# Two edits at the passage from the mixing stage to the experts: where the low parts of x are computed, and which PSUM banks the first projections use

## The chip, the cores and the metric

The kernel runs on one core of a Trainium2 chip. The metric is device microseconds of one execution, lower is better. Five engines work side by side and are kept in step by semaphores: TensorE (PE in the profile; its weight loads are PEld), VectorE (DVE), ScalarE (ACT), GpSimd (POOL) and SyncE (SP), which issues the loads from and stores to memory.

## The reference, cut to what matters

Three stages follow each other on a tensor of 4 batches, 576 tokens and 512 channels. First, sparse attention over 8 heads (half of them local, half strided) gives x. Second, a mixing stage: rotation angles `theta = x @ w_theta`, products of x with their cosine and sine, mixing over tokens, a channel product with a ReLU. Third, four attention experts with a gate:

```
logits = x @ w_gate                      # two of the four experts are kept
for e in range(4):
    q, k, v = x @ wq[e], x @ wk[e], x @ wv[e]
    a  = softmax(causal(q @ k.T / 8))    # 576 x 576 per batch
    ye = a @ v @ wo[e]
    out += gate[e] * ye
```

## The kernel before, in words

x is held transposed, as `X[b]`: 4 chunks (c = 0 to 3) of 128 channels by 576 tokens, for each of the batches b = 0 to 3. Nearly every product is made of three matmuls: each fp32 factor is split into a high part rounded to the matmul's format and a low part, the rest (`mm3`, lines 263 to 266: high by high, high by low, low by high).

`split_act` (L252) splits one chunk of 128 by 576. The high part is a copy: on ScalarE (L256) once all four batches have been split for the mixing stage, on VectorE before that. The low part is a subtraction (L260), and line 259 chooses its engine. `xsplit` is a dictionary that holds one entry for each batch already split. It is empty at the first split, and holds 4 entries when the splits for the experts are made; for those, VectorE takes chunks 0 and 2 and GpSimd takes chunks 1 and 3. Four splits are made for the experts: batch 0 at line 443, inside the last part of the mixing stage; batches 1, 2 and 3 in `project_v` (L465), that is, inside the experts' work for the batch ahead.

The mixing stage ends with `channels(3)` (L361), whose tiles `g` are evicted by VectorE at L371. Then the PSUM pool of that stage is closed and the pool `ps2` (L450) opens, with 8 banks in four tags: `acc` with 2 (projections, output products), `s` with 3 (scores), `t` with 2 (transposes of the weights p), `o` with 1 (attention output).

Line 707 runs nine units of work before the first attention: five of `project_v(0)` (a unit is 12 matmuls for 128 tokens and 260 columns: V of four experts and the gate's logits) and four of `project_qk(0, 0)` (12 matmuls each, 288 tokens of q or of k for two experts). A unit takes one PSUM bank of tag `acc`, which is free again when it has been evicted. For V that is a copy on ScalarE (L494), a subtraction on VectorE (L495) and a copy of the logits on VectorE (L496) into the tile `lg`, which GpSimd has cleared (L469); the fifth unit is copied out whole first (L490), because it serves two batches. For q it is, for each of two halves, a scaled copy on ScalarE (L546) and a subtraction on VectorE (L547); for k, a copy on ScalarE (L550), a subtraction on VectorE (L551) and a copy on GpSimd (L552). GpSimd's queue holds six clearings of the `klow` tiles (L460) ahead of the first clearing of `lg`.

In the experts' stage, `attention` takes one expert of one batch through five tiles of tokens: scores `s` (L596 to L599), row maxima (L601), exponentials (L612), scaling (L619, GpSimd or VectorE), transposes into `tp` (L622), the split of the transposed weights (L630, L631), and the products with V (L574, L578). Between them, lists named `fill` place units of the projections for the batch to come and of the output of the batch behind, each behind the scores of its tile. The order of every engine's instructions is fixed when the program is built, by a planner that simulates the engines; an engine works through its own list strictly in order.

Of the kernel before, what the change touches and what calls it, by code (L numbers as in the profile page):

```python
# [12 lines left out]
F32 = mybir.dt.float32  # L13
# [10 lines left out]
B, S, DM, HD, NE = 4, 576, 512, 64, 4  # L24
# [23 lines left out]
def fused_kernel(ctx: ExitStack, tc: tile.TileContext, ql, kl, vl, qs, ks, vs, wth, wtk, wch, wqk, wvg, wo, out):  # L48
    nc = tc.nc

    def f(ap):
        return ap.bitcast(F32)
# [32 lines left out]
    for rw in (LQ, RQ):  # L85
        t = wb.tile([128, 2, rw], BF16, name=f"twice{rw}")
# [165 lines left out]
    def split_act(x, name):  # L252
        hi = act.tile([128, S], F32R, tag="ahi", name=f"{name}_hi")
        lo = act.tile([128, S], F32R, tag="alo", name=f"{name}_lo")
        if len(xsplit) == B:
            nc.scalar.copy(hi, x)  # L256
        else:
            nc.vector.tensor_copy(hi, x)  # L258
        eng = nc.vector if not xsplit or len(xsplit) == B and name.endswith(("0", "2")) else nc.gpsimd
        halved[name] = eng.tensor_tensor(lo, x, f(hi), op=ALU.subtract).ins  # L260
        return hi, lo

    def mm3(ps, ahi, alo, bhi, blo, first, last):
        nc.tensor.matmul(ps, ahi, bhi, start=first, stop=False)  # L264
        nc.tensor.matmul(ps, ahi, blo, start=False, stop=False)  # L265
        return nc.tensor.matmul(ps, alo, bhi, start=False, stop=last)  # L266

    def split_x(b):
        return [split_act(X[b][:, c, :], f"x{len(xsplit)}_{b}_{c}") for c in range(4)]

    sins, turns = {}, {}
    xsplit, trig, z = {}, {}, {}
# [177 lines left out]
    ps2 = ctx.enter_context(tc.tile_pool(name="ps2", bufs=2, space=PSUM))  # L450


    xproj, vs, qks, moved = {}, {}, {}, []
    identr, mask_cr = (cw.tile([128, 128], F32R, name=name) for name in ("identr", "mask_cr"))
    nc.vector.tensor_copy(identr, ident)
    nc.vector.tensor_copy(mask_cr, mask_c)
# [7 lines left out]
    def project_v(b):  # L464
        xproj[b] = xsplit[0] if b == 0 else split_x(b)  # L465

        vc = cp.tile([128, NT, NE, 2, HD], F32R, tag="vc", name=f"vc_{b}")
        lg = cp.tile([128, NT, 4], F32, tag="lg", name=f"lg_{b}")
        nc.gpsimd.memset(lg, 0.0)  # L469

        nc.gpsimd.memset(f(vc[64:128, NT - 1]), 0.0)
        vs[b] = vc, cp.tile([128, NT, 4], F32, tag="gt", name=f"gt_{b}")
        if b % 2 == 0:

            xe_hi, xe_lo = (cp.tile([128, S], F32R, tag=tag, name=f"xe{tag}_{b}")[:, :512].rearrange(
                "p (c w) -> p c w", c=4) for tag in ("ohi", "olo"))
            for i in range(2):
                x, sl = X[b + i][:, :, 512:S], slice(64 * i, 64 * i + 64)
                nc.scalar.copy(xe_hi[:, :, sl], x)
                nc.vector.tensor_tensor(xe_lo[:, :, sl], x, f(xe_hi[:, :, sl]), op=ALU.subtract)  # L480

        def unit(t):
            w, t0 = TW[t], 128 * t
            if t < 4 or b % 2 == 0:
                pv = ps2.tile([128, 512], F32, tag="acc", name=f"pv_{b}_{t}")
                for c in range(4):
                    xhi, xlo = (v[:, t0:t0 + 128] for v in xproj[b][c]) if t < 4 else (xe_hi[:, c, :], xe_lo[:, c, :])
                    mm3(pv[:, :260], xhi, xlo, wvg_hi[:, c, :], wvg_lo[:, c, :], c == 0, c == 3)
                if t == 4:
                    nc.scalar.copy(v_end, pv[64:128, :260])  # L490
            else:
                pv = v_end
            v = pv[:w, :256].rearrange("p (e d) -> p e d", e=NE)
            nc.scalar.copy(vc[:w, t, :, 0, :], v)  # L494
            nc.vector.tensor_tensor(vc[:w, t, :, 1, :], v, f(vc[:w, t, :, 0, :]), op=ALU.subtract)  # L495
            nc.vector.tensor_copy(lg[:w, t, :], pv[:w, 256:260])  # L496
            if t == NT - 1:
                gates(b, lg)

        return unit  # L500

    def gates(b, lg):
        gt = vs[b][1]

        cnt = cp.tile([128, NT, 4], F32, tag="cnt", name=f"cnt_{b}")
        cmp = cp.tile([128, NT, 4], F32, tag="cmp", name=f"cmp_{b}")
        nc.gpsimd.memset(cnt, 0.0)
        for j in range(4):
            for e0, e1, op in ((0, j, ALU.is_gt), (j + 1, 4, ALU.is_ge)):
                if e0 < e1:  # L510
                    nc.vector.tensor_tensor(cmp[:, :, e0:e1], lg[:, :, j:j + 1].to_broadcast([128, NT, e1 - e0]),
                                            lg[:, :, e0:e1], op=op)
                    nc.vector.tensor_tensor(cnt[:, :, e0:e1], cnt[:, :, e0:e1], cmp[:, :, e0:e1], op=ALU.add)
        mx = cp.tile([128, NT, 2], F32, tag="mx", name=f"mx_{b}")
        nc.vector.tensor_reduce(mx[:, :, 0], lg, axis=AX.X, op=ALU.max)
        nc.vector.tensor_tensor(lg, lg, mx[:, :, 0:1].to_broadcast([128, NT, 4]), op=ALU.subtract)
        nc.scalar.activation(gt, lg, AF.Exp)
        nc.vector.tensor_scalar(cnt, cnt, 1.5, None, op0=ALU.is_lt)
        nc.vector.tensor_tensor(gt, gt, cnt, op=ALU.mult)
        nc.vector.tensor_reduce(mx[:, :, 1], gt, axis=AX.X, op=ALU.add)  # L520
        nc.vector.tensor_scalar_add(mx[:, :, 1], mx[:, :, 1], 1e-9)
        nc.vector.reciprocal(mx[:, :, 1], mx[:, :, 1])
        nc.vector.tensor_tensor(gt, gt, mx[:, :, 1:2].to_broadcast([128, NT, 4]), op=ALU.mult)
# [3 lines left out]
    def project_qk(b, m):  # L527
        q = [cp.tile([128, S], F32R, tag="q", bufs=6, name=f"q_{b}_{m}_{i}") for i in range(2)]
        k = [cp.tile([128, S], F32R, tag="k", bufs=5, name=f"k_{b}_{m}_{i}") for i in range(2)]
        kl = klow[(2 * b + m) % 3]  # L530
        for i in range(2):
            qks[b, 2 * m + i] = (q[i], k[i], kl[i])

        def unit(part, n):
            ms = slice(256 * m + 128 * part, 256 * m + 128 * part + 128)
            sc = 1.0 / math.sqrt(HD) if part == 0 else 1.0
            sl = slice(HALF * n, HALF * (n + 1))
            pq = ps2.tile([128, 512], F32, tag="acc", name=f"pq_{b}_{m}_{part}_{n}")
            for c in range(4):
                mm3(pq[:, :HALF], wqk_hi[:, c, ms], wqk_lo[:, c, ms], xproj[b][c][0][:, sl], xproj[b][c][1][:, sl],  # L540
                    c == 0, c == 3)
            for i in range(2):
                own, other = slice(64 * i, 64 * i + 64), slice(64 - 64 * i, 128 - 64 * i)
                ps = pq[own, :HALF]
                if part == 0:
                    nc.scalar.activation(q[i][own, sl], ps, AF.Copy, scale=sc)  # L546
                    nc.vector.scalar_tensor_tensor(q[i][other, sl], ps, sc, f(q[i][own, sl]), op0=ALU.mult,  # L547
                                                   op1=ALU.subtract)
                else:
                    moved.append(nc.scalar.copy(k[i][own, sl], ps).ins)  # L550
                    nc.vector.tensor_tensor(kl[i][own, sl], ps, f(k[i][own, sl]), op=ALU.subtract)  # L551
                    nc.gpsimd.tensor_scalar(k[i][other, sl], f(k[i][own, sl]), 1.0, 1.0, op0=ALU.mult, op1=ALU.mult)  # L552

        return unit
# [235 lines left out]
```

## Time and profile before

| quantity | value |
|---|---|
| runs | 560.03, 561.43, 562.27 us, median 561.43 |
| profiled execution | 563.35 us, span 561.5 us, mean granted clock 0.979 |
| busy PE, PEld | 532.7 us (95%), 509.5 us (91%) |
| busy DVE, ACT, POOL | 398.9 us (71%), 316.3 us (56%), 199.2 us (35%) |
| passage and experts' stage | about 344.5 us to the end |

The span runs from the first to the last instruction. A busy PE in this table says that matmuls were in flight, not that they ran at full rate: where the granted clock is 0.5 the same matmul takes about twice as long. The mixing stage fills TensorE almost without gaps; the gaps lie in the first 80 us, in the passage and in the experts' stage.

### The profile page before, as it was taken

Reading aid. Unit: us, or ns where it says so; the run is one execution under the profiler, and the core shown is the slowest. Engines: PE = TensorE matmul, PEld = TensorE weight load, DVE = VectorE, ACT = ScalarE, POOL = GpSimd, SP = SyncE. Lnnn points to the kernel's source line nnn. Section 1 sums busy time; section 2 is a strip of 40 time slices with the busy share of each in tenths; the row PEclk is TensorE's granted clock in tenths of the full one; section 3 lists DMA queues with packets and bytes.
Section 4 is the critical chain, followed back from the end, with each engine's and each line's share of the span. In section 5 each row is a group of like instructions: output and inputs, shape, how many; then the busy total and the mean of one; then the engine's idle time right before and its main releaser. Section 6 shows DMA issues by size and latency. Waiting matters only on the chain.

```text
span 561.5 us, 12501 instructions
## 1 busy us (share of the span) xinstructions
PE 532.7 (95%) x4536; PEld 509.5 (91%) x4536; DVE 398.9 (71%) x1210; ACT 316.3 (56%) x904; POOL 199.2 (35%) x285
## 2 busy tenths in 40 slices
PE   6878889999999999999999999989999999999988
PEld 5768889998999999999999998879989999999977
DVE  4858998585856476865456543797988898888972
ACT  4957975436362154352245421585688667767872
POOL 3330013230634112561006443264455444625451
PEclk9959999999999999999999999998999999999998
DMA  9938153360202131000100011000001001100112
GB/s 292 331 99 312 43 169 125 116 232 20 87 17 72 33 123 39 24 24 5 53 0 1 12 48 39 1 1 2 1 10 57 22 2 44 43 2 11 40 37 85
DMA packets 20389, 37.53 MB, mean 67 GB/s; under 512 B 2904, under 2 KB 12296, under 8 KB 20328
## 3 DMA queue, kind: packets, MB, share of 16 engines
q1 hardware_dynamic: 20328, 36.73, 20.1%
q8 instruction: 36, 0.59, 0.4%
q14 instruction: 25, 0.20, 0.1%
HBM read 32.01 MB, written 4.72 MB: 65 GB/s over the span
## 4 chain that ended last, share of the span: by engine, by line
PE 68%; DVE 15%; ACT 6%; POOL 2%; issue 2%; DMA 2%; DVEq 0%; POOLq 0%; ACTq 0%
PE y L264 6%; PE y L266 6%; PE y L265 6%; PE av L242 4%; PE s L189 3%; PE th L264 3%; PE th L266 3%; PE g L264 3%; PE tp L622 3%; PE g L266 3%; PE g L265 3%; PE th L265 3%; PE tp L219 2%; DVE nm L601 2%; PE o L578 2%
## 5 line engine op out<-in xcount | busy, mean ns | idle before, releaser
L264 PE MATMUL y<-wtk_hi,zhi 128*128 128x288 f32 x288 | 85.8, 299 | 1.3 <-DVE X L349 0.8
L265 PE MATMUL y<-wtk_lo,zhi 128*128 128x288 f32 x288 | 85.7, 298 | 0.0
L266 PE MATMUL y<-wtk_hi,zlo 128*128 128x288 f32 x288 | 85.5, 298 | 0.0
L216 POOL TENSOR_TENSOR p<-p,sm 128x288 f32<-128x288 f32 (+2 forms) x48 | 33.3, 700 | 144.2 <-DVE sm L215 57.8
L619 POOL TENSOR_SCALAR p<-p,sm,gt 128x256 f32<-128x256 f32 (+1 forms) x64 | 45.2, 709 | 53.7 <-DVE sm L617 35.2
L612 ACT ACTIVATE p<-s,nm 128x128 f32<-128x128 f32 (+2 forms) x96 | 49.5, 518 | 14.4 <-DVE nm L601 7.9
L264 PEld LDWEIGHTS y<-wtk_hi,zhi 128*128 128x128 f32 x288 | 54.0, 188 | 2.1 <-DVE X L349 1.3
L334 POOL TENSOR_TENSOR zlo<-cs,zhi 128x512 fp32r<-128x512 f32 (+1 forms) x30 | 35.8, 1205 | 54.0 <-DVE zhi L330 43.3
L265 PEld LDWEIGHTS y<-wtk_lo,zhi 128*128 128x128 f32 x288 | 54.1, 188 | 0.1
L266 PEld LDWEIGHTS y<-wtk_hi,zlo 128*128 128x128 f32 x288 | 54.0, 188 | 0.2
L264 PE MATMUL th<-wth_hi,x_hi 128*128 128x256 f32 (+1 forms) x160 | 47.5, 298 | 2.7 <-DVE cs L288 2.2
L601 DVE TENSOR_REDUCE nm<-s 128x1 f32<-128x128 f32 (+2 forms) x96 | 44.3, 469 | 5.4 <-PE s L599 4.4
L265 PE MATMUL th<-wth_lo,x_hi 128*128 128x256 f32 (+1 forms) x160 | 45.7, 287 | 0.0
L266 PE MATMUL th<-wth_hi,x_lo 128*128 128x256 f32 (+1 forms) x160 | 45.3, 288 | 0.1
L223 ACT COPY pt<-tp 96x384 f32<-96x384 f32 (+2 forms) x44 | 20.9, 477 | 41.9 <-PE tp L219 41.5
L189 PE MATMUL s<-k,q 128*108 128x54 f32 (+2 forms) x320 | 43.1, 277 | 1.4 <-DMA k<-in_kl 1.4
L189 PEld LDWEIGHTS s<-k,q 128*108 128x108 f32 (+1 forms) x320 | 40.9, 198 | 3.4 <-issue 3.2
L260 POOL TENSOR_TENSOR x_lo<-X,x_hi 128x576 fp32r<-128x576 f32 x20 | 29.6, 1484 | 33.1 <-DVE x_hi L258 26.4
L264 PE MATMUL pq<-x_hi,wqk_hi 128*128 128x288 f32 x128 | 39.8, 311 | 1.0 <-DVE q L547 0.7
L264 PE MATMUL g<-u_hi,wch_hi 128*128 128x288 f32 x128 | 38.7, 303 | 1.4 <-DVE X L371 1.4
L631 DVE TENSOR_TENSOR ptlo<-tp,pthi 128x128 fp32r<-128x128 f32 (+4 forms) x80 | 37.7, 479 | 1.1 <-ACT pthi L630 0.6
L265 PE MATMUL pq<-x_lo,wqk_hi 128*128 128x288 f32 x128 | 37.9, 296 | 0.0
(172 smaller groups left out, 1704.8 us busy)
## 6 DMA issues: line engine op xcount, KB each, us to landing
X<-in_wtk SPq DMA_DIRECT2D x18, 287.8 KB
q<-in_qs SPq DMA_DIRECT2D x8, 594.0 KB
q<-in_ql SPq DMA_DIRECT2D x8, 576.0 KB
v<-in_vl SPq DMA_DIRECT2D x24, 144.0 KB
out_t<-X SPq DMA_DIRECT2D x20, 128.0 KB
k<-in_kl SPq DMA_DIRECT2D x8, 304.0 KB
k<-in_ks SPq DMA_DIRECT2D x8, 288.0 KB
X<-in_wth SPq DMA_DIRECT2D x8, 255.8 KB
```

What stands on the lines that cost most here:

```text
L189: nc.tensor.matmul(s[:rm, i * kw:i * kw + w], qt[:, j0 + i, :], kt[:, k0:k0 + w], start=False, stop=i == n - 1)
L216: nc.gpsimd.tensor_tensor(tiles(p), tiles(p), each(sm), op=ALU.mult)
L242: nc.tensor.matmul(av[64 * h:64 * h + 64, c0:c0 + wi], vg[:w, i, h, :], pt[:w, i, h, :wi], start=True, stop=True)
L260: halved[name] = eng.tensor_tensor(lo, x, f(hi), op=ALU.subtract).ins
L264: nc.tensor.matmul(ps, ahi, bhi, start=first, stop=False)
L265: nc.tensor.matmul(ps, ahi, blo, start=False, stop=False)
L266: return nc.tensor.matmul(ps, alo, bhi, start=False, stop=last)
L334: halved[b, h] = eng.tensor_tensor(lo, zf, f(hi), op=ALU.subtract).ins
L601: nc.vector.tensor_reduce(nm[:w, t + ci:t + ci + 1], s[:w, :c1 - c0], axis=AX.X, op=ALU.max, negate=True)
L612: nc.scalar.activation(p[:w, c0:c1], scs[ci][:w, :c1 - c0], AF.Exp, bias=nm[:w, t:t + 1], scale=1.0, accum_out=acc)
L619: eng.tensor_scalar(p[:w, :kn], p[:w, :kn], sm[:w, t:t + 1], gt[:w, t, e:e + 1], op0=ALU.mult, op1=ALU.mult)
L631: nc.vector.tensor_tensor(dst(ptlo), src, f(dst(pthi)), op=ALU.subtract)
```

## The change

Two edits. The low parts of all splits for the experts go to VectorE, chunks 1 and 3 as well, in all four batches. And the projections take their PSUM tile from a function `place`, which hands out the tags `t, t, s, s, s, acc, acc` to the first seven units, in the order in which units are written, and `acc` to all later ones. Nothing else differs in the source; the planner orders the new program anew.

```diff
@@ split_act
-        eng = nc.vector if not xsplit or len(xsplit) == B and name.endswith(("0", "2")) else nc.gpsimd
+        eng = nc.vector if len(xsplit) in (0, B) else nc.gpsimd
@@ before project_v
+    free = ["t", "t", "s", "s", "s", "acc", "acc"]
+
+    def place(name):
+        tag = free.pop(0) if free else "acc"
+        return ps2.tile([128, 512], F32, tag=tag, bufs=3 if tag == "s" else 2, name=name)
+
@@ project_v, unit
-                pv = ps2.tile([128, 512], F32, tag="acc", name=f"pv_{b}_{t}")
+                pv = place(f"pv_{b}_{t}")
@@ project_qk, unit
-            pq = ps2.tile([128, 512], F32, tag="acc", name=f"pq_{b}_{m}_{part}_{n}")
+            pq = place(f"pq_{b}_{m}_{part}_{n}")
```

## Rows read from the trace of the kernel before

**Rows 1.** What TensorE waited for from 344 us on: total, times, longest, in us.
```profile
PE pv L266 <- DVE x_lo L260: 2.1, 2, 1.2
PE pq L264 <- DVE q L547: 0.7, 1, 0.7
```
**Rows 2.** Timeline of TensorE in the passage: start, duration, in brackets idle time before.
```profile
345.11 0.39 PE L264 MATMUL pv<-wvg_hi,x_hi 128*128 128x260 f32 x1 [0.55 <-DVE X L371]
...
347.85 0.28 PE L265 MATMUL pv<-wvg_lo,x_hi 128*128 128x260 f32 x1
347.97 0.28 PE L266 MATMUL pv<-wvg_hi,x_lo 128*128 128x260 f32 x1
348.78 0.36 PE L264 MATMUL pv<-wvg_hi,x_hi 128*128 128x260 f32 x1 [0.53 <-DVE lg L496]
...
356.35 0.29 PE L266 MATMUL pq<-x_hi,wqk_lo 128*128 128x288 f32 x1
357.35 0.37 PE L264 MATMUL pq<-x_hi,wqk_hi 128*128 128x288 f32 x1 [0.70 <-DVE q L547]
```
**Rows 3.** Timelines of GpSimd, VectorE and ScalarE in the passage.
```profile
344.68 3.70 POOL L460 MEMSET klow<- 64x576 f32 x6 [12.99 <-PE g L266]
348.47 0.16 DVE L496 COPY lg<-pv 128x4 f32<-128x4 f32 x1 [0.79 <-POOL lg L469]
353.39 0.37 ACT L490 COPY v_end<-pv 64x260 f32<-64x260 f32 x1 [1.08 <-PE pv L266]
354.97 0.41 ACT L546 ACTIVATE q<-pq 64x288 fp32r<-64x288 f32 x1 [0.52 <-PE pq L266]
```
**Rows 4.** Timelines of the split of batch 1: GpSimd, VectorE, TensorE.
```profile
373.07 1.41 POOL L260 TENSOR_TENSOR x_lo<-X,x_hi 128x576 fp32r<-128x576 f32 x1 [0.72 <-ACT x_hi L256]
375.47 1.42 POOL L260 TENSOR_TENSOR x_lo<-X,x_hi 128x576 fp32r<-128x576 f32 x1
373.57 1.53 DVE L260 TENSOR_TENSOR x_lo<-X,x_hi 128x576 fp32r<-128x576 f32 x1
375.02 1.14 DVE L601 TENSOR_REDUCE nm<-s 128x1 f32<-128x384 f32 x2
376.09 1.42 DVE L260 TENSOR_TENSOR x_lo<-X,x_hi 128x576 fp32r<-128x576 f32 x1
375.15 0.39 PE L266 MATMUL pv<-wvg_hi,x_lo 128*128 128x260 f32 x1 [0.95 <-DVE x_lo L260]
377.56 0.58 PE L266 MATMUL pv<-wvg_hi,x_lo 128*128 128x260 f32 x1 [1.15 <-DVE x_lo L260]
```
**Rows 5.** Stretches: length, busy PE, PEld, DVE, ACT, POOL (instructions), granted clock, DMA, GB/s.
```profile
361.00:373.90 12.90, 12.78 (x99) 12.21 (x98) 11.61 (x38) 11.16 (x33) 8.28 (x13) 1.00 0.01 2
373.90:377.50 3.60, 1.56 (x10) 1.06 (x9) 3.60 (x5) 3.14 (x10) 2.82 (x3) 0.94 0.00 0
377.50:384.00 6.50, 6.44 (x29) 6.27 (x30) 4.54 (x19) 2.42 (x8) 2.56 (x5) 0.51 0.00 0
47.50:49.60 2.10, 0.00 (x0) 0.00 (x0) 1.87 (x6) 1.16 (x4) 0.00 (x0) 1.00 1.04 402
```
**Rows 6.** Timelines of the splits of batches 2 and 3 on VectorE, and of TensorE.
```profile
430.39 0.76 DVE L260 TENSOR_TENSOR x_lo<-X,x_hi 128x576 fp32r<-128x576 f32 x1
431.72 1.41 DVE L260 TENSOR_TENSOR x_lo<-X,x_hi 128x576 fp32r<-128x576 f32 x1 [0.21 <-ACT x_hi L256]
437.86 0.36 PE L264 MATMUL pv<-wvg_hi,x_hi 128*128 128x260 f32 x1
481.50 1.58 DVE L260 TENSOR_TENSOR x_lo<-X,x_hi 128x576 fp32r<-128x576 f32 x1 [0.34 <-ACT x_hi L256]
```
**Rows 7.** The same stretches as in rows 5, around the splits of batches 2, 3 and 0.
```profile
428.00:440.00 12.00, 11.45 (x90) 10.80 (x89) 10.96 (x30) 10.36 (x29) 7.74 (x12) 1.00 0.15 51
478.00:490.00 12.00, 11.91 (x92) 11.12 (x91) 10.22 (x30) 10.02 (x29) 7.63 (x12) 1.00 0.15 51
298.00:308.00 10.00, 10.00 (x82) 10.00 (x81) 6.58 (x13) 7.12 (x18) 5.83 (x5) 1.00 0.00 0
```

## The prediction

> **What bounds the kernel now.** The waits of TensorE come first, because it is busy through most of the span. From 344 us to the end they are few, and the largest is on the operation that the change moves: the third matmul of a V unit waits for low parts of x, 2.1 us in two waits; 0.7 us are lost on the bank of a q unit [rows 1]. The timeline of TensorE in the passage gives the places. The first V unit starts at 345.11 after 0.55 us for the last eviction of the mixing stage. The third loses 0.53 us to the copy of the logits, and the first k unit 0.70 us to the second subtraction of q [rows 2]. The other engines say why: GpSimd clears `klow` for 3.70 us before it clears `lg`, so VectorE's first logits copy waits until 348.47, and the bank of the first unit is held by it. Further on ScalarE waits for TensorE twice, 1.08 and 0.52 us: between the third V unit and the first q unit TensorE is late, not the evictions [rows 3]. Then comes the split of batch 1: TensorE stands 0.95 and 1.15 us for low parts 0 and 2, both on VectorE [rows 4]. Last, the table of stretches: VectorE is full there (3.60 of 3.60 us), and after it the granted clock is at the lower level, 1.2 GHz, for 6.5 us; before, it was at 2.4 GHz [rows 5].
>
> **The banks.** Units 1 to 5 are V, 6 and 7 are q, 8 and 9 are k. Before, with two banks, unit 3 waits for unit 1. After, units 3 to 7 find a bank that nobody has used. The last matmuls of unit 2 start 0.12 us apart (347.85, 347.97), and unit 3 begins at 348.78: 0.81 instead of 0.12, so 0.69 us go, and 0.08 us with them for the long first matmul of a resumed stream (0.36 against 0.28). Together 0.77 us [rows 2]. All the way to the first q unit the evictions have room, by the 1.08 and 0.52 us that ScalarE waits [rows 3], so the gain reaches it whole. What is late next: unit 8 takes the bank of unit 6 and unit 9 that of unit 7, as before, since only seven units get banks of their own and both q units sit in `acc`. The wait of 1.00 us between starts at 356.35 and 357.35 thus stays, only earlier. The bounds: 0 if the attention behind takes the gain back, and 1.64 us if also unit 8's excess goes (1.00 less 0.13 for a pitch of these wider units, an estimate from 0.12 by 288 over 260 columns). I take 0.77, since nothing in the rows shortens the eviction of q. The first unit's 0.55 us stays: it waits for the mixing stage, not for a bank of the new pool. The planner's new order is the part that no row prices; the nearest row, one wait of this stretch, is 0.5 to 0.7 us, either way.
>
> **The low parts, batch 1.** Alone a low part takes 0.76 us on VectorE [rows 6], and 1.42 on GpSimd [rows 4]. Both VectorE ones here took 1.53 and 1.42, and each overlaps one on GpSimd: the first began at 373.57, GpSimd's ran until 374.48, and 375.10 is 0.62 us after that [rows 4]. So it mostly stood still. The Trainium skill (SBUF — State Buffer, section "SBUF: two separate sides") says that VectorE with two SBUF inputs and GpSimd take one pair of ports in turn, each for a whole instruction. The trace agrees by those 0.62 us; were the speed shared instead, two added low parts would cost VectorE about 1.5 us each, not 0.76.
>
> Now VectorE alone, in the order that stands there, with each low part that GpSimd loses put behind its neighbour. Low 0 from 373.57 to 374.33; low 1 to 375.09; the two maxima take 1.07 (375.02 to 376.09), to 376.16; low 2 to 376.92; low 3 to 377.68 [rows 4]. Four times 0.76 is 3.04 us against the 2.95 of two stretched ones: VectorE pays 0.09 us. TensorE gets low 0 at 374.33 and not at 375.10, and low 2 at 376.92 and not at 377.51. The second decides, since the V unit can't end before it: 0.59 us gained. Low 3 comes at 377.68, while some 0.8 us of other matmuls stand before its use in the old order. Bounds: 1.5 us gained (all four in a row from 373.57 end at 376.61, with low parts only 0.76 apart, so that TensorE has two matmuls for most of each gap), and 1.0 lost (the maxima put off by 1.5 us delay the exponentials, and 0.5 comes back). I take 0.59.
>
> **The clock behind it.** From 377.5 to 384.0 the granted clock is 0.51, with 6.44 us busy on TensorE [rows 5]. At the upper level the same work is some 3.3 us. But VectorE has 4.54 us of work in that stretch, and it was full before; so without the drop the stretch is bounded by VectorE: 6.50 less 4.54, 1.96 us saved. Does the drop go? It follows a stretch in which TensorE was busy 1.56 of 3.60 us. After, it stands perhaps 1.7 of 3.0 us, in three pieces. The row at 47.5 shows 2.10 us without one matmul and a clock of 1.00 through it [rows 5], so such a gap need not bring a drop. I take it as gone, by a small margin: bounds 0 and 3.2 us.
>
> **Low parts, batches 2, 3 and 0.** For batch 2, VectorE has 0.76 and 1.41 us now and would have 3.04: 0.87 more. TensorE wants V only at 437.86, some 5 us after the last of them [rows 6]. VectorE is busy 10.96 of 12 us there and TensorE 11.45, so little room hides it [rows 7]; against it, GpSimd loses 2.84 us and delivers its scalings of p and its copies of k earlier. Batch 3 likewise: 0.81 (as batch 2's short one) and 1.58 become 3.04, 0.65 more, with TensorE busy 11.91 of 12 [rows 6, 7]. Batch 0 falls in the mixing stage, where TensorE is busy 10.00 of 10 and VectorE 6.58: two more low parts make 8.1 at most [rows 7], hidden by the token products; if that cover went, 0.7. I take 0 for all three, bounds 1.0 gained (GpSimd's queue) and 1.5 lost (0.87 and 0.65 on the path).
>
> **The sum.** The profiled execution took 563.35 us, 561.5 of span and 1.85 around it. Less 0.77, 0.59 and 1.96: 3.3 us, so 560.0 for such an execution. The median of the runs is 561.43, 1.92 lower, so 558.1 for the median. Its own range, from the bounds near it: 556.3 to 559.4.
>
> **Rivals.** *The clock falls all the same* (0.27). The waits are rearranged and about as long in sum. For: they shrink by only 0.6 of 2.1 us. Against: the gap at 47.5. Then 0.77 and 0.59 remain: 560.1.
>
> *The gain is given back* (0.13). From 361.0 to 373.9 VectorE is busy 11.61 of 12.90 and TensorE 12.78 [rows 5]. If the first attention is paced by VectorE's list, being early at 355 is worth nothing; if in addition low 2 comes where it came, nothing remains: 561.3. For: the chain there is mostly VectorE. Against: VectorE's own list starts earlier with the evictions.
>
> *Slower* (0.15). VectorE is the fullest helper in the experts' stage, and it gets 0.87 and 0.65 us more for batches 2 and 3. Its row maxima and reciprocals stand behind four low parts, TensorE runs out of scores and transposes near 433 us, where the stretch already leaves it 0.55 us idle [rows 7], and the clock falls there too, for 6.5 us at half rate, 3.25 us. Sum: 0.87 and 0.65 and 3.25, less 0.77: 4.0 slower, 565.4. It decides itself where a second gap of about 1 us follows the one of 0.55; without the fall of the clock it is 0.75 slower, 562.2. For: batch 1 shows the price. Against: V of batch 2 is not wanted until 5 us later.
>
> *The source does not bring it about* (0.05). The planner puts the low parts where the old order stood still anyway, or fills `t` and `s` late: 561.4.
>
> **Numbers.** My forecast has 0.40. A measurement of this kernel tells about 0.5% from no change, 2.8 us, so the line for faster is 558.6. Of my own case about three quarters lies under it, 0.31, and of the others 0.06 (both GpSimd's relief and a shorter gap): faster 0.37. Slower takes the part of its rival in which the clock falls, and a badly planned order: 0.12. The rest, 0.51, is the same. The range of 8 in 10 cuts off the best and the worst tenth: 555.9 to 562.8.
>
> **What would show it.** In the trace after: the third V unit starts 0.12 us behind the second, and ScalarE's waits of 1.08 and 0.52 us remain; the first k unit still waits for VectorE's `q`. No low part above 0.9 us on VectorE, none on GpSimd behind the mixing stage. At the split of batch 1 TensorE waits about 1.5 us for low parts, and the clock stays at 1.00. I am wrong if the clock falls there or at another place, if VectorE's maxima come later around 433 us and TensorE waits for them, or if the first k unit no longer waits.

## The result, and the profile after

The changed kernel is slower. Its median is 563.57 us (20 runs, 562.33 to 566.45) beside 559.79 us (20 runs, 556.22 to 562.99) for the kernel before; the ratio is 1.0081, with an interval from 1.0063 to 1.0099, so some 4.5 us (the two medians lie 3.8 us apart). I had forecast 558.1 us and a gain. The profiled execution took 565.61 us (span 563.5, mean granted clock 0.972). GpSimd's busy time fell from 199.2 to 184.8 us; VectorE's did not rise (397.8 after 398.9 us).

The timeline of TensorE in the passage, after (start, duration, idle before in brackets):

```profile
346.39 0.39 PE L264 MATMUL pv<-wvg_hi,x_hi 128*128 128x260 f32 x1 [0.55 <-DVE X L371]
...
349.13 0.28 PE L265 MATMUL pv<-wvg_lo,x_hi 128*128 128x260 f32 x1
349.25 0.28 PE L266 MATMUL pv<-wvg_hi,x_lo 128*128 128x260 f32 x1
349.37 0.28 PE L264 MATMUL pv<-wvg_hi,x_hi 128*128 128x260 f32 x1
...
356.76 0.29 PE L266 MATMUL pq<-x_hi,wqk_lo 128*128 128x288 f32 x1
357.85 0.37 PE L264 MATMUL pq<-x_hi,wqk_hi 128*128 128x288 f32 x1 [0.80 <-DVE q L553]
```

The third V unit starts at 349.37, 0.12 us behind the last matmul of the second; the wait for the logits of [rows 2] is gone, the first unit's 0.55 us and the first k unit's wait are there. This is what the prediction described. The low parts of batch 1, on VectorE, and TensorE's one wait for them that is listed:

```profile
374.07 0.74 DVE L260 TENSOR_TENSOR x_lo<-X,x_hi 128x576 fp32r<-128x576 f32 x1
375.20 0.74 DVE L260 TENSOR_TENSOR x_lo<-X,x_hi 128x576 fp32r<-128x576 f32 x1
376.47 0.74 DVE L260 TENSOR_TENSOR x_lo<-X,x_hi 128x576 fp32r<-128x576 f32 x1
377.50 0.74 DVE L260 TENSOR_TENSOR x_lo<-X,x_hi 128x576 fp32r<-128x576 f32 x1
375.99 0.39 PE L266 MATMUL pv<-wvg_hi,x_lo 128*128 128x260 f32 x1 [0.51 <-DVE x_lo L260]
```

0.74 us each, where [rows 4] had 1.53 and 1.42. So the two parts of the change do at their own places much of what was said, with less waiting for low parts (0.5 us listed) than the 1.5 us named. The loss is elsewhere. What TensorE waited for, after (total, times, longest, in us): the first row from 300 to 345 us, the others from 344 us on.

```profile
PE y L266 <- POOL zlo L334: 1.0, 1, 1.0
...
PE s L602 <- ACT p L618: 1.5, 3, 0.8
PE s L602 <- POOL k L558: 1.4, 1, 1.4
PE pq L264 <- DVE q L553: 1.0, 2, 0.8
PE pv L266 <- DVE x_lo L260: 0.5, 1, 0.5
```

The 2.1 us for `x_lo` of [rows 1] have become 0.5, but two waits for GpSimd stand out: 1.4 us for k, which was 0.2 us before, and 1.0 us in the mixing stage, where TensorE had not waited for GpSimd at all. Both come with another order of the lists. The timeline of GpSimd at the end of the mixing stage, after:

```profile
320.20 3.78 POOL L104 TENSOR_TENSOR wqk_lo<-wqk_st,wqk_hi 128x512 fp32r<-128x512 f32 x3 [0.74 <-ACT wqk_hi L102]
323.93 0.72 POOL L334 TENSOR_TENSOR zlo<-cs,zhi 128x256 fp32r<-128x256 f32 x1
```

and before:

```profile
319.81 2.54 POOL L104 TENSOR_TENSOR wqk_lo<-wqk_st,wqk_hi 128x512 fp32r<-128x512 f32 x2 [0.75 <-ACT wqk_hi L102]
322.31 0.95 POOL L334 TENSOR_TENSOR zlo<-cs,zhi 128x256 fp32r<-128x256 f32 x1
323.23 1.27 POOL L104 TENSOR_TENSOR wqk_lo<-wqk_st,wqk_hi 128x512 fp32r<-128x512 f32 x1
```

Three splits of weights, not two, stand ahead of the last low part of z, which the token products wait for. No instruction here is one that the change touches. The second place is the split of batch 2 (ScalarE, VectorE, GpSimd, TensorE, after):

```profile
430.59 1.24 ACT L256 CAST x_hi<-X 128x576 fp32r<-128x576 f32 x2
431.73 0.40 ACT L556 CAST k<-pq 64x288 fp32r<-64x288 f32 x1
432.04 0.74 DVE L260 TENSOR_TENSOR x_lo<-X,x_hi 128x576 fp32r<-128x576 f32 x1
432.20 0.86 POOL L558 TENSOR_SCALAR k<-k 64x288 fp32r<-64x288 f32 x1 [3.84 <-DVE sm L623]
433.12 1.20 PE L602 MATMUL s<-k,q 128*128 128x384 f32 x3 [1.36 <-POOL k L558]
```

A copy of k stands behind two copies of x on ScalarE, GpSimd's second copy follows it, and TensorE's next scores need that one. This copy took 0.86 us beside a low part on VectorE; nearly all others of its kind take 0.43, so about 0.4 of the 1.36 us is GpSimd's own lengthened time. The clock fell right behind it, and not at batch 1 (columns as in [rows 5]):

```profile
377.50:384.00 6.50, 5.96 (x44) 5.30 (x44) 5.68 (x24) 2.90 (x10) 2.56 (x5) 1.00 0.01 1
433.50:437.50 4.00, 4.00 (x19) 3.68 (x18) 2.96 (x7) 0.71 (x3) 1.25 (x3) 0.59 0.14 47
```

To see which differences are of the kernel and which of an execution, I cut each profile at the same matmuls: A, from the start of the last matmul of the angles to that of the last token product; B, the passage, from the first V matmul to the first score; C, from the first V matmul of batch 1 to that of batch 2; D, the same from batch 2 to batch 3; E, from the start of the last q or k matmul to TensorE's end. Each number is the difference of two times in the timelines; * marks a stretch in which the clock fell. Each ratio compares a kernel with runs of the kernel before taken beside it (their medians are 559.49 to 560.00 us), so it is not the quotient of two medians of this table.

| kernel | median us | ratio to before, interval | A | B | C | D | E |
|---|---|---|---|---|---|---|---|
| before | 559.79 | | 30.15 | 15.87 | 64.17* | 49.15 | 32.21* |
| after | 563.57 | 1.0081 (1.0063 to 1.0099) | 31.77 | 15.10 | 64.94* | 50.92 | 31.14 |
| e1 banks alone | 558.62 | 0.9963 (0.9942 to 0.9984) | 30.16 | 15.12 | 61.56 | 49.21 | 31.15 |
| e2 lows alone | 563.45 | 1.0062 (1.0034 to 1.0090) | 31.78 | 15.89 | 63.41 | 50.97 | 31.13 |
| e3 lows of batch 0 | 561.42 | 1.0026 (1.0002 to 1.0050) | 31.77 | 15.88 | 61.61 | 49.18 | 31.20 |
| e4 lows of batches 1 to 3 | 562.90 | 1.0042 (1.0020 to 1.0065) | 30.16 | 15.89 | 63.40 | 50.94 | 32.08* |
| e5 lows, old order | 559.44 | 1.0001 (0.9977 to 1.0026) | 30.15 | 15.90 | 61.98 | 49.02 | 32.07* |
| e6 before, new order | 566.54 | 1.0125 (1.0097 to 1.0153) | 31.65 | 15.88 | 65.72* | 50.94 | 32.20* |
| e7 after, old order | 558.91 | 0.9971 (0.9951 to 0.9992) | 30.16 | 15.10 | 61.99 | 49.01 | 32.18* |
| e8 after, z first | 562.09 | 1.0049 (1.0022 to 1.0077) | 30.51 | 15.11 | 63.41 | 50.92 | 31.13 |
| e9 banks, lows of 1 and 3, old order | 558.42 | 0.9980 (0.9956 to 1.0005) | 30.17 | 15.10 | 61.37 | 49.01 | 31.14 |
| e10 after, GpSimd's old order | 559.96 | 0.9998 (0.9969 to 1.0026) | 30.57 | 15.12 | 62.63 | 49.77 | 31.15 |
| e11 e9 with eight banks | 557.74 | 0.9966 (0.9944 to 0.9988) | 30.17 | 13.66 | 61.40 | 49.02 | 31.15 |

Without a fall of the clock, stretch C takes 61.6 us in before's order (e1, e3) and 63.4 in the changed kernel's (e2, e8). The change is then 1.62 (A) less 0.77 (B) plus 1.8 (C) plus 1.8 (D): 4.4 us, and the measured ratio says 4.5, the medians 3.8. The two profiled executions lie only 2.0 us apart in span because the one of before had two falls of the clock and the one of after had one.

### The profile page after: what moved, and what is told of

It reads as the page before. It is cut to its first block, busy times and chain, and to the rows that moved or that the text cites. A ratio compares the mean times of both kernels' runs of the same rounds, so it can differ in the third digit from the quotient of the medians.

```text
span 563.5 us, 12477 instructions
## 1 busy us (share of the span) xinstructions
PE 537.4 (95%) x4536; PEld 511.1 (91%) x4536; DVE 397.8 (71%) x1218; ACT 315.9 (56%) x904; POOL 184.8 (33%) x277
## 4 chain that ended last, share of the span: by engine, by line
PE 72%; DVE 13%; ACT 7%; DMA 4%; issue 2%; POOL 1%; SPq 0%; DVEq 0%; ACTq 0%; POOLq 0%
PE y L264 6%; PE y L266 6%; PE y L265 6%; PE s L189 4%; PE av L242 4%; PE tp L219 3%; PE tp L628 3%; PE g L264 3%; PE g L265 3%; PE g L266 3%; PE th L264 3%; PE th L266 3%; PE pq L264 2%; PE th L265 2%; PE o L584 2%
## 5 line engine op out<-in xcount | busy, mean ns | idle before, releaser
L216 POOL TENSOR_TENSOR p<-p,sm 128x288 f32<-128x288 f32 (+2 forms) x48 | 30.4, 639 | 146.7 <-DVE sm L215 64.4
L607 DVE TENSOR_REDUCE nm<-s 128x1 f32<-128x128 f32 (+3 forms) x96 | 44.2, 468 | 5.2 <-PE s L605 3.4
L266 PE MATMUL pq<-x_hi,wqk_lo 128*128 128x288 f32 x128 | 38.0, 297 | 0.0
L266 PE MATMUL g<-u_hi,wch_lo 128*128 128x288 f32 x128 | 37.9, 296 | 0.0
```

Of the source, the lines that this page charges most:

```text
L216: nc.gpsimd.tensor_tensor(tiles(p), tiles(p), each(sm), op=ALU.mult)
L607: nc.vector.tensor_reduce(nm[:w, t + ci:t + ci + 1], s[:w, :c1 - c0], axis=AX.X, op=ALU.max, negate=True)
```

## The experiments

**e1 to e4: one part alone.** The change has two edits; the second acts on four batches.

```
# e1: place() and its two calls alone
# e2: line 259 alone
+        eng = nc.vector if len(xsplit) in (0, B) else nc.gpsimd
# e3 (e4): that for batch 0 ("123" for "0": batches 1 to 3) alone
+        eng = nc.vector if not xsplit or len(xsplit) == B and (name.endswith(("0", "2")) or name[3] in "0") else nc.gpsimd
```

> The bank edit alone; every engine's instructions stand in the order of the kernel before. Theory A (the loss is all from the low parts, the bank edit keeps its 0.77 us): 0.8 us faster than before, 0.6 to 1.0, ratio 0.9986. Rival B (the gain at the third V unit is taken back in the first attention): within 0.3 us of before. Rival C (other banks for acc, s and t cost something themselves): 1 us or more slower.

> The low parts alone, all four batches, banks as before. Theory A: slower than before by the loss of the whole change and the 0.8 us of the banks, 5.3 us in all (4 to 6.5), ratio 1.0095. Rival B or C: slower by 3 to 4.5 us, as the whole change is, or less.

> Low parts on VectorE for batch 0 alone, banks as before. Theory A1 (the split in the mixing stage lets the planner put a third weight low part on GpSimd ahead of the last zlo, for which TensorE waits 1.0 us): 1.6 us slower (1.0 to 2.0), first V unit 1.2 to 1.7 us later than before. Rival A2 (all the loss lies in the experts' stage, VectorE's extra load there): same as before within 0.4 us.

> Low parts on VectorE for batches 1, 2 and 3, batch 0 as before, banks as before. Theory A1: the rest of the loss, 3 to 4 us slower, most of it between 430 and 480 us. Rival A2: all of it, 5 us. If the split of batch 0 is the whole cause: within 0.5 us of before.

The table gives the answer: the banks alone are a gain, the low parts alone are the loss, batch 0's edit makes that of A and the other three make those of C and D (which of the three makes which was not separated). Not every size came as expected. By the ratios e1 gains 2.1 us (0.9 to 3.2) and not 0.8, while e2 and e4 lose 3.5 and 2.4 us, less than the 5.3 and the 3 to 4 of theory A. The stretches without a fall of the clock give 0.77 for e1 and 5.2 for e2. Falls of the clock could make up part of the difference: the mean granted clock was 0.9847 over e1's runs, 0.9835 over e2's and 0.9821 over those of before beside them, which in 560 us is about 1.5 and 0.8 us (an estimate). That either edit causes this is not shown.

The lists say something that the times don't: with the banks alone the planner leaves every engine's order as it was, while with the lows it makes a new one; of the 3338 rows of TensorE's list before (equal neighbours in one), a comparison with the list of e2 marks 284. In D the loss does not even stand at the moved instructions: from the first V matmul of batch 2 to the first copy of x for batch 3 it is 43.59 us in e2 and 43.55 after, beside 41.77 before; the rest of D, with the low parts of batch 3, is 7.38, 7.37 and 7.38 us. e1 also bears on the clock. What TensorE waited for from 344 us on in e1:

```profile
PE pv L266 <- DVE x_lo L260: 2.1, 2, 1.2
```

and a stretch that holds the second of the two waits and 4 us behind it (columns as in [rows 5]):

```profile
374.00:380.50 6.50, 5.22 (x42) 4.80 (x41) 6.38 (x21) 3.39 (x11) 3.19 (x5) 1.00 0.00 0
```

The same 2.1 us of waiting as before the change, the same list, and the clock stays at 1.00 (in e3 too).

**e5 to e7: the order, or VectorE's work.** If VectorE's extra work were the cause, the loss would stay whatever the order; if the new order is, it would go with it. So the order of TensorE, VectorE, ScalarE and GpSimd was written out as edges between neighbours, and the planner placed only the moved low parts, mostly right behind their neighbours (the edit in outline):

```
+    for engine, names in ORDER.items():      # the lists of another kernel, as planned there
+        for one, two in zip(names, names[1:]):
+            tc.add_manual_dep(traced[two], one, issue_order_only)
# e5: e2 with the lists of before   e6: before with the lists of e2   e7: after with the lists of before
```

> All low parts on VectorE, the banks as before, and the order of TensorE, ScalarE, VectorE and GpSimd written out as it stood before, so that only the eight moved instructions change their engine (the planner puts each into VectorE's list, mostly right behind its neighbour). The order theory says that the loss of 3.5 us (the lows alone, 563.45) is not VectorE's work but the new order that the planner made: this kernel is back at 559 to 560.3 us, mixing stage without the 1.6 us, and 49.2 us (not 51.0) from the third V of batch 2 to that of batch 3. The load theory says that four low parts in a row delay VectorE's maxima and copies whatever the order: 562.5 to 564 us, with the 1.8 us in each of the two stretches still there.

> The inverse: low parts on GpSimd and VectorE as before, banks as before, but the order of all four engines written out as the planner made it for the kernel with all lows on VectorE. The order theory: it loses what that kernel lost, 563 to 564.5 us (a little more than 563.45 if GpSimd's longer low parts now hold what the order wants early), with the 1.6 us in the mixing stage and some 1.8 us in both stretches behind it. The load theory: no loss, 559.5 to 560.5 us.

> The whole change (banks and all lows on VectorE) with the order of before written out. The order theory: the banks give their 0.77 and the fall of the clock at the split of batch 1 comes more rarely, so 557.5 to 559 us, as the banks alone (558.62) or up to 0.6 under it. The load theory: as the changed kernel less nothing, 562.5 to 564 us. If the clock falls more often where four lows stand in a row, between the two.

Both directions agree. With the old order the low parts cost nothing that can be measured (1.0001); with the new one, before loses even more than e2 did (566.54 us, expected were 563 to 564.5), though its low parts are on the engines where they were. What TensorE waited for in C and D of e6:

```profile
PE s L596 <- POOL k L552: 2.2, 2, 2.0
PE pv L266 <- DVE x_lo L260: 1.6, 2, 0.9
PE s L596 <- ACT p L612: 1.3, 2, 0.8
```

The longest wait for k is 2.0 us here and 1.4 in e2, because GpSimd still has low parts of its own in front of it. The load theory is out as the cause of the 5.2 us.

e7 keeps a loss of 0.4 us in C against e1, and its place is the split of batch 2. GpSimd and VectorE there in e7, with the wait of TensorE:

```profile
427.36 1.83 POOL L625 TENSOR_SCALAR p<-p,sm,gt 128x256 f32<-128x256 f32 x1 [4.03 <-PE tp L628]
429.28 0.94 POOL L558 TENSOR_SCALAR k<-k 64x288 fp32r<-64x288 f32 x2
427.08 0.74 DVE L260 TENSOR_TENSOR x_lo<-X,x_hi 128x576 fp32r<-128x576 f32 x1
428.10 0.74 DVE L260 TENSOR_TENSOR x_lo<-X,x_hi 128x576 fp32r<-128x576 f32 x1
429.76 0.44 PE L602 MATMUL s<-k,q 128*128 128x384 f32 x1 [0.78 <-POOL k L558]
```

and in e1:

```profile
419.60 0.56 POOL L625 TENSOR_SCALAR p<-p,sm,gt 128x256 f32<-128x256 f32 x1 [3.58 <-DVE sm L623]
427.65 1.41 DVE L260 TENSOR_TENSOR x_lo<-X,x_hi 128x576 fp32r<-128x576 f32 x1 [0.21 <-ACT x_hi L256]
428.43 1.06 POOL L625 TENSOR_SCALAR p<-p,sm,gt 128x256 f32<-128x256 f32 x1
429.58 0.43 POOL L558 TENSOR_SCALAR k<-k 64x288 fp32r<-64x288 f32 x1
430.06 0.45 PE L602 MATMUL s<-k,q 128*128 128x384 f32 x1 [0.23 <-POOL k L558]
```

The same scaling of p takes 0.56 us alone, 1.06 beside the last part of one low part on VectorE, as in e1, and 1.83 beside two of them, as in e7. The 0.77 us between e1 and e7 are about one low part of 0.74. The prediction had GpSimd's scalings and copies of k come earlier, since GpSimd has less to do; here GpSimd stands while VectorE's low parts run. The Trainium skill (SBUF — State Buffer, section "SBUF: two separate sides") says that VectorE with two SBUF inputs and GpSimd hold their shared ports in turn, each for the whole of an instruction. The prediction priced only the half of this rule that is a gain for VectorE; the 0.56, 1.06 and 1.83 us agree with the other half. One thing it leaves open: in e7 the scaling had begun at 427.36, before the second low part at 428.10, and yet that low part took 0.74 us and the scaling stood.

**e8 to e10: single places.**

```
# e8: after, the weights of the experts split behind the last low part of z
-                with tc.issue_after(turns[b, 1]):
+                with tc.issue_after(turns[b, 1]), tc.issue_after(halved[b, 1]):
# e9: e7, but line 259 takes VectorE for all chunks in batches 1 and 3 only
# e10: after, with GpSimd's list alone written out as before
```

> The changed kernel with one order put right: GpSimd gets the splits of wqk and wvg only behind the last low part of z (zlo) of the fourth batch; the order of TensorE and VectorE is the changed kernel's, ScalarE's differs in a few copies there. If the 1.62 us that the mixing stage lost are the third split of wqk ahead of that zlo, the stage gets 1.3 to 1.6 us back and the kernel takes 562.0 us, with TensorE's two waits of some 1.0 us for zlo gone; the two stretches of 1.8 us behind stay. Rival: the loss there is the later transposes of xn, or wqk now comes late for the first q unit: nothing gained, 563.5 us or more.

> The banks, and all low parts on VectorE for batches 1 and 3 alone (0 and 2 as before), with the order of before written out. With all four batches the stretch from the split of batch 2 to its V took 0.54 us more than with the banks alone, since GpSimd's scaling of p there lasted 1.83 us and not 1.06 beside two low parts on VectorE, and its copy of k came that much later. If that is the cause, the 0.54 goes and the other stretches stay as in that kernel: 558.0 to 558.6 us, ratio 0.995 to 0.997. Rival: the 0.54 comes from batch 1's new pace, and stays: 558.9 us, as with all four.

> The changed kernel, with GpSimd's order alone written out as before (less the moved low parts); the planner orders TensorE, VectorE and ScalarE anew around it. If GpSimd's queue carries the loss (zlo behind wqk, the copies of k behind other work), it is back at 558.5 to 560 us. If the places on TensorE, VectorE and ScalarE carry the 1.8 us of both later stretches, only the mixing stage's 1.6 go: 561.5 to 562.5 us.

In e8 one instruction of GpSimd moves ahead of three (and a few copies on ScalarE move), A falls from 31.77 to 30.51, and TensorE's listed wait for zlo is gone. GpSimd in e8:

```profile
318.64 0.74 POOL L334 TENSOR_TENSOR zlo<-cs,zhi 128x256 fp32r<-128x256 f32 x1 [0.80 <-DVE zhi L330]
319.38 3.77 POOL L104 TENSOR_TENSOR wqk_lo<-wqk_st,wqk_hi 128x512 fp32r<-128x512 f32 x3
```

That is 1.26 of the 1.62 us; 0.36 of A stay with the rest of the new order. C and D stay at 63.41 and 50.92, as expected. e9 takes the low parts of batch 2 back to GpSimd, and the piece from the first copy of x for batch 2 to its first V matmul falls from 8.98 us in e7 to 8.35 (8.44 in e1): the cause was as named. Its ratio of 0.9980 lies above the 0.995 to 0.997 expected, and its median does not separate it from e7. In e10, with GpSimd's list alone held as before, most of the loss goes: A is 30.57, C 62.63, and the median 559.96 us, where before stands. Its D of 49.77 holds eight matmuls (0.8 us) that stand behind D in the other kernels. From the first V matmul of batch 2 to the last q or k matmul e10 takes 88.99 us, before 88.88 and after 90.66, so there the loss is gone. In all some 3.6 of the 5.2 us go. The planner orders the other engines anew around GpSimd's list, so e10 does not say that GpSimd's own instructions cost all of that.

**e11: the eighth bank.** The prediction said that the first k unit goes on waiting, since it takes the first q unit's bank.

```
-    free = ["t", "t", "s", "s", "s", "acc", "acc"]
+    free = ["t", "t", "s", "s", "s", "acc", "acc", "o"]      # e9 otherwise
```

> The kernel before this one (banks, all lows on VectorE for batches 1 and 3, the order of before) with the bank of the values as an eighth bank of the passage, so that the first k unit takes a bank that nobody has used and not that of the first q unit. The prediction said that the wait of the first k unit stays with seven banks because both q units sit in the same two; if the bank is all it waits for, the 0.82 us before it go, the scores of the first attention begin 0.8 to 0.95 us sooner after the first V unit (14.2 instead of 15.1 us), and the time is 557.2 to 558 us, ratio 0.9955 to 0.998. If the values of the first head now wait for that bank, or the evictions of q on ScalarE and VectorE bound the k units anyway, nothing is gained: 558.4 us.

The wait is gone, and B falls by 1.44 us, more than the 0.95 expected. But the next piece, from the first score to the split of batch 1, takes 1.2 us more (11.89 for 10.68 us in e9): the scores now wait 0.5 us for `klow` and the transposes 0.5 us for GpSimd's p, and the first attention does not run sooner for it. Only about 0.2 us remain in the profile. The median, 557.74 us, is the lowest of all kernels run, but its interval does not part it from e1 or e9.

## Why the prediction was wrong

**The step that failed** is the order. The low parts were priced "in the order that stands there", and "I take 0 for all three" put those of batches 2, 3 and 0 at nothing, with bounds of 1.0 gained and 1.5 lost. I had the planner's new order as a part that "no row prices", but only under the banks, where it did not change at all, and at one wait of 0.5 to 0.7 us. The runs showed a new order that costs 1.62 us in A (the edit of batch 0) and 1.8 in C and 1.8 in D (the edits of batches 1 to 3, not separated), 5.2 in all. With the old order the same low parts cost nothing that can be measured (e5), and with the new one the kernel loses though the low parts stay (e6). The durations on VectorE were right, and they were put into a list that was no longer there.

**The clock behind batch 1**, −1.96 us, was the largest term and is mis-sized. The clock did not fall there after the change, as I had said, but it does not fall in e1 and e3 either, whose waits are those of before. The profiled execution of before was one in which it fell: C took 64.17 us there against 61.6. I credited the change with what belongs to one execution. I then took the 1.96 off the median of the runs, although I had just counted that median as 1.92 us below this execution, so part of the fall may have been taken off twice. Over all runs the mean granted clock is 0.9821 before (the 104 runs beside e1 to e11) and 0.9833 after (20), which in 560 us is about 0.7 us (an estimate), and whether even that is the change's doing is not shown. The base was off in the same direction: 561.43 us, a median of three runs, against 559.79 over twenty.

**The banks**, −0.77 us: right. B goes from 15.87 to 15.10, the third unit follows without a pause, and the wait of the first k unit stays until it gets a bank of its own (e11). That e1's time gained more than 0.77 us is not explained by B. The bound "the attention behind takes the gain back" did not hold for 0.77, but it held for most of the next 1.44.

**The low parts of batch 1**, −0.59 us: right at its place in the old order, and given back behind it. TensorE's waits for them were 0.5 us after the change and 1.0 in e7, not about 1.5. In e1 the last wait for low parts ends 3.85 us after the first V matmul of batch 1, in e7 3.06: 0.79 us sooner. At the first copy of x for batch 2 that is 53.01 us against 53.12, so 0.1 is left. This is the second rival's mechanism, one stretch further on.

**The duration of a low part**, 0.76 us alone: right for 14 of 16 after the change (0.74 to 0.76); two of batch 3 took 0.80 and 0.97, one of them above the 0.9 that I had named as a limit. The costs of 0.87 and 0.65 us that I named for batches 2 and 3 if they fell on the path measured 0.54 (8.98 less 8.44) and −0.1 (7.27 in e7 less 7.40 in e1, from the first copy of x for batch 3 to its V) at the old order, and the 0.54 came as GpSimd's lengthened time.

**The rival that ends slower** had the right place and a part of the mechanism: TensorE ran out of work at the split of batch 2 and, in that profile, the clock fell. But it named VectorE's maxima as late, and it was the second copy of k on GpSimd. That its 565.4 us came near the measured 563.57 is luck: its terms are others. Against it I had written that V of batch 2 is wanted 5 us later; this was no argument, since TensorE waited there for k and not for V.

What stays open: in C the listed waits of TensorE are hardly longer in e2 than in e5 (3.3 against 3.2 us), and yet C takes 1.43 us more. In both C holds the same 437 matmuls. By the start of each matmul to that of the next, less its columns at 2.4 GHz, the pauses of 0.1 to 0.5 us sum to 7.9 us in e2 (45) and 5.2 in e5 (32), those above 0.5 to 3.2 (3) and 4.0 (6). So the loss there lies in many small pauses; which moves in the list make them was not tried. Nor was it shown why the planner prefers this order.

## What to carry to other kernels

Where a planner lays out the lists, an edit that gives an instruction to another engine is two edits; compare the planned lists first, and time the edit at the old order as well. A fall of the clock in one profile is not the kernel's until other executions show it too: cut several profiles at the same matmuls, and the stretches that agree to 0.05 us tell the rest apart. An instruction taken from GpSimd and put on VectorE can return as GpSimd's own time, if what stays there runs beside it.

## What the runs showed of the hardware

A gap of about the same length brings a fall of the clock in one execution and none in another with the same order (e2 differs from the changed kernel in the banks alone). After the change TensorE stood 1.36 us for k and the clock went to 0.59 in the four microseconds behind. In e2, with the same wait (1.4 us), the stretch with the wait and the one behind:

```profile
427.90:432.00 4.10, 2.74 (x20) 2.28 (x20) 4.07 (x12) 4.10 (x12) 1.12 (x2) 1.00 0.00 0
432.00:436.00 4.00, 4.00 (x31) 3.85 (x30) 3.57 (x10) 2.19 (x8) 1.34 (x3) 1.00 0.23 80
```

In C such a fall cost 1.5 us (64.94 against 63.41) and 2.6 us (before, 64.17 against 61.6), and about 1.0 in E. It is not most of the 6 us by which single runs of one kernel differ: 28 of the 104 runs of before had the same mean granted clock, 0.984, and took 557.4 to 563.6 us. What else differs between them is open.
